# Scaling and casting w_out on GpSimd, with the second half requested by SyncE

## The chip, the cores and the metric

The kernel runs on one core of a Trainium2 chip. The metric is the device time of one execution in microseconds, the median of several. The engines are named as in the profile: PE is TensorE, DVE is VectorE, ACT is ScalarE, POOL is GpSimd, SP is SyncE.

## The reference

A global filter along the sequence (a real Fourier transform, a product with a complex filter, the inverse transform) is followed by two dense layers with a snake activation between them.

```
x: (8, 3008, 256); filt_r, filt_i: (1505, 256)
X = rfft(x, axis=1); Y = X * (filt_r + 1j * filt_i); y = irfft(Y, n=3008, axis=1)
x2 = y.reshape(24064, 256)
h = x2 @ w_in                              # w_in: (256, 2048)
s = sin(alpha * h)                         # alpha: (2048,)
g = h + s * s / (alpha + 1e-09)
out = g @ w_out                            # w_out: (2048, 256), out: (24064, 256) float32
```

## The kernel before

The work is split by linearity. Since g has a part that is linear in h, the kernel computes out = (s * s) @ (w_out / alpha) + x2 @ (w_in @ w_out). The first factor on the right is held as `w_out2` (float16, 16 blocks of 128 rows), the product w_in @ w_out as `m_t`. For `m_t` it needs w_out itself in float16, `w_out16`, and the transpose of w_in, `w_inT`.

The Fourier transform is done as small matrix products in stages (`f1`, `f2x`, `product`, `f2g`, `f3`), one pass for each of the 8 sequences of the batch. The first sequence is worked alone on the chip (`f1_chip`, `turn1`, `g_chip`, `turn2`); it is the prologue. The other seven are cut into small steps which a hand-written table, `plan`, puts into slots of the main loop. The main loop runs over 47 chunks g of 512 tokens with 8 slots q each. In slot 8 * g + q stand, in this order: one `mlp_in` (two matmuls into a bank of the pool `psh`, and the sine on ACT), a part of `mlp_out` of the chunk before (matmuls with `w_out2` as the moving side, L290), the planned steps, a second `mlp_in` and a second part of `mlp_out`; in every second slot `square` on DVE (L278) squares four blocks of the sine. The order on every engine is that of the code; each engine works through its queue in that order and waits at an instruction until its inputs are there.

w_out comes in two halves of 1024 rows, in float32, into one staging buffer: the pool `stp` has one buffer under the tag `st`, which both halves and later the two halves of w_in in float32 share in turn. So the second half can be requested only when all readers of the first are done. `load_w_out(h, eng)` (L346) requests half h on the queue of `eng`; `prep_w_out(h, k)` (L354) scales four of its blocks by `recip`, which is 1 / (alpha + 1e-9), on DVE; `cast_w_out(h)` (L351) casts the half on POOL. The first half is requested in the prologue on SP's queue, after the first half of w_in has landed. Its cast, its two `prep_w_out` and the request of the second half on POOL's queue stand in slots 6 and 7; the second half is scaled and cast in slot 10, and `prep_m` (L373) multiplies w_in by w_out16 in slot 13. `mlp_out` of chunk 0 uses blocks 0 to 15 of `w_out2` in turn, from slot 8 on.

In the same slots stand the steps of the second sequence: from slot 5 to slot 10 up to three `f1` steps each (L141, into a bank of the pool `psf` of three; even steps are evicted by ACT, odd ones by DVE, L142), and one `prep_w_inT` (L367, another `psf` bank, evicted by ACT and DVE in turn, L370). After `f1` steps 7 and 15 SP stores `asb` to DRAM (L146); `shuffle1` reads it back from slot 10 (L196). `load_x(1, 4)` puts eight loads on POOL's queue at the end of the prologue.

Of the kernel before, what the change touches and what calls it, by code (L numbers as in the profile page):

```python
# [63 lines left out]
def kernel(  # L64
# [10 lines left out]
    nc = tc.nc  # L75
# [3 lines left out]
    def dram(ap, off, dims):  # L79
        return bass.AP(tensor=ap.tensor, offset=ap.offset + off, ap=dims)  # L80
# [34 lines left out]
    w_out2 = cpool.tile([128, 16, C], FP16, name="w_out2")  # L115
# [5 lines left out]
    def gate(ins, earlier):  # L121

        tc.add_manual_dep(ins.ins, earlier.ins.name, mybir.DependencyInfo(
            mybir.DependencyClass.Sync, mybir.DependencyReason.DATA), reason="order of transfers")

    def load_x(b, parts=2):

        xt[b] = (xbpool if b else vpool).tile([GT, RP, C], FP16, name="xt", tag="xb" if b else "vt")
        n = RP // parts
        for h in range(parts):  # L130
            for p0, p1 in ((0, 80), (80, GT)):
                x_dma[b, h] = nc.gpsimd.dma_start(  # L132
                    out=xt[b][p0:p1, n * h:n * h + n, :],
                    in_=dram(x, (b * S + RP * p0 + n * h) * C, [[RP * C, p1 - p0], [1, n * C]]))
# [14 lines left out]
    def f1_chip(k):  # L149

        for half in range(2):
            ps = (psf if half else psh).tile([128, 4, 4 * NK], FP32, name="psa0", tag="f" if half else "ph")
            for i in range(4):
                nc.tensor.matmul(out=ps[:, i, :], lhsT=xt[0][:, 4 * k + i, 128 * half:128 * half + 128],
                                 rhs=wa2, start=True, stop=True)
            (nc.vector.tensor_copy if half else nc.scalar.copy)(
                out=a_c[:, half, :, 16 * k:16 * k + 16].rearrange("p s (r a) -> p s r a", a=4),
                in_=ps.rearrange("p r (s a) -> p s r a", a=4))
# [154 lines left out]
    def evict_out(g, h):  # L313
        if h == 0:
            ot[g] = opool.tile([128, 4, C], FP32, name="ot", tag="ot")
        nc.vector.tensor_copy(out=ot[g][:, 2 * h:2 * h + 2, :], in_=po[g, h])  # L316
# [20 lines left out]
    w_inT, w_out32, w_in32, alpha_b = [], [], [], []  # L337

    def prep_alpha():
        ps = pso.tile([128, 2, C], FP32, name="psal", tag="po")  # L340
        nc.tensor.matmul(out=ps[:, 0, 0:16], lhsT=alpha_r, rhs=ident32, start=True, stop=True)
        nc.vector.tensor_copy(out=alpha_t, in_=ps[:, 0, 0:16])
        nc.vector.tensor_scalar(out=recip, in0=alpha_t, scalar1=1e-9, scalar2=None, op0=ALU.add)
        nc.vector.reciprocal(out=recip, in_=recip)
# [6 lines left out]
    def cast_w_out(h):  # L351
        nc.gpsimd.tensor_copy(out=w_out16[:, 8 * h:8 * h + 8, :], in_=w_out32[h])

    def prep_w_out(h, k):  # L354
        for i in range(4 * k, 4 * k + 4):
            nc.vector.tensor_scalar(out=w_out2[:, 8 * h + i, :], in0=w_out32[h][:, i, :],  # L356
                                    scalar1=recip[:, 8 * h + i:8 * h + i + 1], scalar2=None,
                                    op0=ALU.mult)

# [32 lines left out]
    def keep_busy(n, src):  # L392

        ps = psh.tile([128, 2, C], FP32, name="idle", tag="ph")
        for _ in range(n):
            nc.tensor.matmul(out=ps, lhsT=ident[0:src.shape[0]], rhs=src, start=True, stop=True)

    def load_filter(s0, n, earlier=None):

        for f, src in ((0, filt_r), (1, filt_i)):  # L400
            first = nc.gpsimd.dma_start(out=fri[0:32, f, s0:s0 + n, :],
                                        in_=dram(src, s0 * C, [[MT * C, 32], [C, n], [1, C]]))
            if earlier is not None and f == 0:
                gate(first, earlier)
            filter_dma[s0] = nc.gpsimd.dma_start(
                out=fri[32:64, f, s0:s0 + n, :],
                in_=dram(src, (MT - s0) * C, [[MT * C, 32], [-C, n], [1, C]]))
# [10 lines left out]
    def swap_wg(s0, n):  # L418

        cs = slice(128 * s0, 128 * s0 + 128 * n)  # L420
        for p in (0, 64):
            nc.vector.tensor_copy(out=wgs[p:p + 64, cs], in_=wg[64 - p:128 - p, cs])
# [3 lines left out]
    def at(slot, f, *args):  # L426
        plan.setdefault(int(slot), []).append((f, args))
# [25 lines left out]
        for q, u in zip(slots, todo):  # L453
            at(8 * g + q, f3, *u)
    for k in range(2):
        at(6 + k, prep_w_out, 0, k)
        at(10 + k, prep_w_out, 1, k)
        at(13, prep_m, k)
    at(6, cast_w_out, 0)
    at(7, load_w_out, 1, nc.gpsimd)  # L460
    at(10, cast_w_out, 1)
    at(14, load_w_in32, 0)
    at(22, load_w_in32, 1)
    for k in range(8):
# [6 lines left out]
    with tc.manual_schedule():  # L471
        nc.sync.dma_start(out=wa2, in_=wa2_d.ap())
        nc.sync.dma_start(out=ident, in_=id_d.ap())
        nc.scalar.dma_start(out=alpha_r, in_=moe_alpha.rearrange("(a p) -> a p", p=128))
        nc.scalar.dma_start(out=ident32, in_=id32_d.ap())
        nc.scalar.dma_start(out=we2, in_=we2_d.ap())
        nc.scalar.dma_start(out=wa, in_=wa_d.ap())
        nc.scalar.dma_start(out=we, in_=we_d.ap())
        nc.sync.dma_start(out=wb[:, 0:8 * 128], in_=wb_d.ap()[:, 0:8 * 128])
        warm = cpool.tile([128, 1], FP32, name="warm")  # L480
        nc.vector.memset(warm, 0.0)
        nc.scalar.activation(out=warm, in_=warm, func=AFT.Sin)
        load_x(0, 4)
        for s0 in (0, 8, 16):
            load_filter(s0, 8, None if s0 else x_dma[0, 1])
        for h in range(2):
            hs = slice(1024 * h, 1024 * h + 1024)
            for cb in range(2):
                w_in_dma[h, cb] = nc.gpsimd.dma_start(out=w_in16[:, cb, hs],
                                                      in_=moe_w_in[128 * cb:128 * cb + 128, hs])  # L490
        gate(nc.sync.dma_start(out=wg[:, 0:8 * 128], in_=wg_d.ap()[:, 0:8 * 128]), x_dma[0, 2])
        nc.sync.dma_start(out=wb[:, 8 * 128:], in_=wb_d.ap()[:, 8 * 128:])
        gate(nc.sync.dma_start(out=wg[:, 8 * 128:], in_=wg_d.ap()[:, 8 * 128:]), filter_dma[0])
        a_c = vpool.tile([128, 2, NK, 128], FP16, name="a_c", tag="vt")
        prep_alpha()
        for k in range(8):
            f1_chip(k)
            if k == 0:
                keep_busy(3, xt[0][:, 0:2, :])
        bint[0] = xbpool.tile([128, NK, C], FP16, name="bint", tag="xb")  # L500
        wgs = vpool.tile([128, NK * 128], FP16, name="wgs", tag="vt")
        b_c = agpool.tile([128, 2, RP, NK, 4], FP16, name="b_c", tag="ag")
        for t in range(12):
            turn1(t)
            if t in (2, 4, 6, 8, 10, 11):
                f2x(0, (t - 1) // 2)
            if t == 9:
                swap_wg(0, 8)
                fold_filter(0, 8)
        for t in range(16):  # L510
            if t in (4, 8):
                fold_filter(2 * t, 8)
                if t == 4:
                    swap_wg(8, 16)
            if t >= 4:
                g_chip(t // 2 - 2, t % 2)
                if t % 2 and t > 8:
                    keep_busy(2, wg[:, 0:512])
            if 4 <= t < 10:
                f2x(0, t + 2)  # L520
            if t < 12 and t % 2:
                product(0, t // 2, 0)
        gin[0] = ginpool.tile([4 * NK, RP, C], FP16, name="gin", tag="gin")
        for j in range(4):
            turn2(j)
        gate(load_w_out(0, nc.sync), w_in_dma[0, 1])
        load_x(1, 4)
        for i in range(4):
            f3(i // 2, i % 2)

        for g in range(NCH):
            for q in range(8):
                if g and q == 7:
                    evict_out(g - 1, 0)
                mlp_in(g, 2 * q)
                if g:
                    mlp_out(g - 1, q, 1)
                for f, args in plan.get(8 * g + q, ()):
                    f(*args)
                mlp_in(g, 2 * q + 1)  # L540
                if g:
                    mlp_out(g - 1, q, 0)
                if g and q == 7:
                    evict_out(g - 1, 1)
                    store_out(g - 1, 0, 4, (nc.sync,))
                if q % 2:
                    square(g, q)
        out_last(NCH - 1)
# [28 lines left out]
```

## Time and profile before

| what | us |
|---|---|
| median of 3 runs | 839.96 (838.85 to 840.75) |
| the profiled execution | 839.08 |
| its span, first to last instruction | 837.3 |
| PE busy | 813.0 (97%) |
| ACT busy | 620.3 (74%) |
| DVE busy | 515.2 (62%) |
| POOL busy | 36.3 (4%) |

The span and the busy times are those of the profiled execution. The granted clock of PE is 0.997 of full speed over the span. The chain that ended last is 90% PE. The slots in question lie between 48 and 80 us of the span; the chunk loop begins at 39.5 us.

A row of a timeline has the start, the length, the engine, the line, the operation with its tiles, and in brackets the idle time of the engine ahead of it with what ended that. Numbers at the end of names of buffers are left out, so `w_out` stands for `w_out2`, `w_out16` and `w_out32` alike.

### The profile page before, as it was taken

The numbers are of one execution on the slowest core, as the hardware profiler recorded it, in microseconds if no ns is written. First come the engines' busy times: TensorE is split into PE (matmuls) and PEld (weight loads), VectorE is DVE, ScalarE is ACT, GpSimd is POOL, SyncE is SP. The second block draws the span as 40 slices with busy tenths as digits, with TensorE's granted clock in tenths as the row PEclk, the third lists the DMA queues.
The fourth block names the chain that finished last, engine by engine and source line by source line (L and its number), as shares of the span: only waits on it lengthen the run. The fifth ranks groups of instructions, "written<-read, shape, count | busy, mean of one in ns | idle before, by whom it ended". The sixth has DMA issues, their size and how long they took to land.

```text
span 837.3 us, 15277 instructions
## 1 busy us (share of the span) xinstructions
PE 813.0 (97%) x6221; PEld 573.7 (69%) x6221; DVE 515.2 (62%) x683; ACT 620.3 (74%) x1155; POOL 36.3 (4%) x66
## 2 busy tenths in 40 slices
PE   6779999999999999999999999999999999999997
PEld 5547676677767776677767776677766777767665
DVE  4886975676466665566555684567655675443532
ACT  4786987787777786788777887778877787666662
POOL 5301000000000000000000000000000000000000
PEclk9999999999999999999999999999999999999999
DMA  9926385424644163612834146431645233321122
GB/s 197 208 66 244 103 192 113 139 73 103 152 102 126 51 161 89 201 29 75 196 92 140 51 107 169 103 101 51 160 117 144 61 96 95 61 52 26 28 50 50
DMA packets 68134, 91.55 MB, mean 109 GB/s; under 512 B 7224, under 2 KB 52808, under 8 KB 66552
## 3 DMA queue, kind: packets, MB, share of 16 engines
q1 hardware_dynamic: 61792, 71.25, 30.8%
q0 software_dynamic: 5760, 19.14, 11.2%
q8 instruction: 48, 0.79, 0.4%
q10 hardware_dynamic: 512, 0.19, 0.1%
q14 instruction: 22, 0.18, 0.1%
HBM read 58.83 MB, written 46.66 MB: 126 GB/s over the span
## 4 chain that ended last, share of the span: by engine, by line
PE 90%; DVE 5%; DMA 3%; issue 1%; POOL 1%; ACT 0%; DVEq 0%; POOLq 0%
PE po L290 42%; PE ph L271 37%; PE psa L141 2%; PE psy L260 2%; PE psg L232 2%; PE psx L202 2%; DMA w_out<-in_moe_w_out_dram 1%; DVE vt L278 1%; PE pe L304 1%; DMA fri<-in_filt_i_dram 1%; DMA xt<-in_x_dram 1%; DVE gin L189 1%; DVE w_out L356 1%; PE psg L175 0%; DVE z L215 0%
## 5 line engine op out<-in xcount | busy, mean ns | idle before, releaser
L273 ACT ACTIVATE vt<-ph 128x512 f16<-128x512 f32 x688 | 404.5, 601 | 141.9 <-PE ph L271 136.8
L290 PE MATMUL po<-w_out,vt 128*128 128x256 f16 x2944 | 426.6, 272 | 1.4 <-DVE ot L316 0.8
L290 PEld LDWEIGHTS <-vt 128*128 128x128 f16 x2944 | 287.4, 98 | 173.4 <-issue 2.2
L271 PE MATMUL ph<-yt,w_ina 128*128 128x512 f16 x1376 | 399.3, 379 | 0.0
L278 DVE TENSOR_TENSOR vt<-vt 128x2048 f16<-128x2048 f16 x188 | 230.1, 1224 | 196.6 <-ACT vt L273 196.0
L271 PEld LDWEIGHTS <-w_ina 128*128 128x128 f16 x1376 | 128.2, 98 | 32.8
L316 DVE COPY ot<-po 128x512 f32<-128x512 f32 x92 | 63.0, 688 | 22.4 <-PE po L290 21.4
L206 ACT CAST xs<-psx 128x512 f16<-128x512 f32 x96 | 56.6, 592 | 8.2 <-PE psx L202 8.0
L142 DVE CAST asb<-psa 96x512 f16<-96x512 f32 x56 | 38.2, 685 | 33.4 <-PE psa L141 31.6
L234 ACT CAST gsb<-psg 128x512 f16<-128x512 f32 x84 | 49.5, 589 | 12.3 <-PE psg L232 11.2
L290 PE MATMUL po<-m_t,yt 128*128 128x256 f16 x368 | 55.2, 273 | 0.0
L264 DVE CAST yt<-psy 128x240 f16<-128x240 f32 (+45 forms) x92 | 32.2, 351 | 34.3 <-ACT yt L262 33.3
L262 ACT CAST yt<-psy 128x376 f16<-128x376 f32 (+29 forms) x128 | 46.2, 363 | 7.6 <-PE psy L260 0.7
L273 ACT ACTIVATE vt<-ph,alpha_t 128x512 f16<-128x512 f32 x64 | 42.8, 694 | 11.1 <-PE ph L271 10.8
L260 PE MATMUL psy<-we,gin 96*128 96x94 f16 x512 | 42.1, 204 | 1.1 <-ACT asb L142 0.7
L132 POOL DMA_DIRECT2D xt<-in_x_dram x40 | 20.9, 528 | 496.2 <-PE psy L260 287.5
L260 PEld LDWEIGHTS <-gin 96*128 96x128 f16 x512 | 35.6, 97 | 7.7 <-issue 1.5
L290 PEld LDWEIGHTS <-yt 128*128 128x128 f16 x368 | 36.0, 98 | 4.2
L142 ACT CAST asb<-psa 96x512 f16<-96x512 f32 x56 | 32.3, 583 | 8.0 <-PE psa L141 7.9
L202 PE MATMUL psx<-bint,wb 128*128 128x256 f16 x192 | 37.4, 277 | 0.0
L271 PE MATMUL ph<-yt,w_in 128*128 128x512 f16 x128 | 36.4, 379 | 0.2 <-ACT yt L262 0.2
L215 DVE TENSOR_TENSOR z<-xs,fri 128x1024 f16<-128x1024 f16 x48 | 32.9, 686 | 4.6 <-ACT xs L206 4.5
(71 smaller groups left out, 384.1 us busy)
## 6 DMA issues: line engine op xcount, KB each, us to landing
out_dram<-ot SPq DMA_DIRECT2D x109, 128.0 KB
scr<-asb SPq DMA_DIRECT2D x14, 768.0 KB
bint<-scr SPq DMA_DIRECT2D x21, 512.0 KB
scr<-gsb SPq DMA_DIRECT2D x21, 512.0 KB
xt<-in_x_dram POOLq DMA_DIRECT2D x12, 640.0 KB, 8.1
gin<-scr SPq DMA_DIRECT2D x7, 768.0 KB
out_dram<-ot SPq DMA_DIRECT2D x84, 60.0 KB
gin<-scr SPq DMA_DIRECT2D x7, 576.0 KB
```

The costliest lines, as they stand in the source:

```text
L142: (nc.vector.tensor_copy if u % 2 else nc.scalar.copy)(out=asb[b][:, 2 * u:2 * u + 2, :], in_=ps)
L202: nc.tensor.matmul(out=ps[:, i, :], lhsT=wb[:, 128 * (2 * t + i):128 * (2 * t + i) + 128], rhs=bint[b][:, 2 * t + i, :], start=True, stop= ...
L206: nc.scalar.copy(out=xs[b, t // 2][:, t % 2 * 2:t % 2 * 2 + 2, :], in_=ps)
L215: nc.vector.tensor_tensor(out=z[k], in0=xs[b, k], in1=fri[:, 0, k4, :], op=ALU.mult)
L234: nc.scalar.copy(out=gsb[b][:, 2 * t:2 * t + 2, :], in_=ps)
L260: nc.tensor.matmul(out=ps[:, t, :], lhsT=gin[b][:, 4 * a + t, 128 * cb:128 * cb + 128], rhs=we if b else we2, start=True, stop=True)
L262: nc.scalar.copy(out=yt[g][:, cb, :, lo:lo + n], in_=ps[:, :, 0:n])
L271: nc.tensor.matmul(out=ph, lhsT=(w_in16 if g < 4 else w_ina)[:, cb, 128 * jb:128 * jb + 128], rhs=yt[g][:, cb], start=(cb == 0), stop=(cb ...
L273: nc.scalar.activation(out=vt[g][:, jb, :], in_=ph, func=AFT.Sin, scale=alpha_t[:, jb:jb + 1] if g < 4 else 1.0)
L278: nc.vector.tensor_tensor(out=v4, in0=v4, in1=v4, op=ALU.mult)
L290: nc.tensor.matmul(out=po[g, h][:, i, :], lhsT=vt[g][:, k, ts] if k < 16 else yt[g][:, k - 16, t], rhs=w_out2[:, k, :] if k < 16 else m_t[ ...
L316: nc.vector.tensor_copy(out=ot[g][:, 2 * h:2 * h + 2, :], in_=po[g, h])
```

## The change

`prep_w_out` scales a whole half, eight blocks, on POOL instead of four on DVE. The scaling and the cast of the first half stand in the prologue, behind the loads of the second sequence on POOL's queue. The request of the second half stands in slot 1 on SP's queue, and its scaling and cast in slot 1 on POOL. In both halves the scaling is now ahead of the cast.

```
-    def prep_w_out(h, k):
-        for i in range(4 * k, 4 * k + 4):
-            nc.vector.tensor_scalar(out=w_out2[:, 8 * h + i, :], in0=w_out32[h][:, i, :],
+    def prep_w_out(h):
+        for i in range(8):
+            nc.gpsimd.tensor_scalar(out=w_out2[:, 8 * h + i, :], in0=w_out32[h][:, i, :],
                                     scalar1=recip[:, 8 * h + i:8 * h + i + 1], scalar2=None,
                                     op0=ALU.mult)
...
     for k in range(2):
-        at(6 + k, prep_w_out, 0, k)
-        at(10 + k, prep_w_out, 1, k)
         at(13, prep_m, k)
-    at(6, cast_w_out, 0)
-    at(7, load_w_out, 1, nc.gpsimd)
-    at(10, cast_w_out, 1)
+    at(1, load_w_out, 1, nc.sync)
+    at(1, prep_w_out, 1)
+    at(1, cast_w_out, 1)
...
         gate(load_w_out(0, nc.sync), w_in_dma[0, 1])
         load_x(1, 4)
+        prep_w_out(0)
+        cast_w_out(0)
         for i in range(4):
             f3(i // 2, i % 2)
```

## The prediction

> **What bounds the kernel now.** I read the page first: TensorE (PE) is busy 97% of the span at full granted clock, so a change pays only where PE stands idle. The stretches of busy time say where that is near the changed code.
>
> ```profile
> 50.00:55.00 5.00, 3.65 (x25) 2.08 (x25) 4.07 (x10) 3.95 (x8) 0.00 (x0) 1.00 0.00 0
> 55.00:60.00 5.00, 3.47 (x25) 1.90 (x23) 4.79 (x11) 4.11 (x9) 0.96 (x1) 1.00 0.57 144
> 60.00:65.00 5.00, 4.76 (x38) 3.19 (x36) 2.94 (x5) 3.68 (x7) 0.00 (x0) 1.00 0.71 218
> 65.00:70.00 5.00, 4.38 (x40) 3.12 (x39) 4.22 (x9) 3.44 (x6) 1.90 (x1) 1.00 0.62 165
> 70.00:75.00 5.00, 5.00 (x51) 4.14 (x49) 2.87 (x5) 2.63 (x6) 0.00 (x0) 1.00 0.68 247
> ```
>
> The columns are length, then busy time of PE, weight loads, VectorE (DVE), ScalarE (ACT) and GpSimd (POOL). From 50 to 70 us PE is idle 1.35 + 1.53 + 0.24 + 0.62 = 3.74 us; from 70 to 100 it is full. So a microsecond that PE wins before 70 should reach the end, and there are fewer than four to win. The chain of waits through this window:
>
> ```profile
> 54.29 1.05 DVE w_out L356 x4
> 55.34 0.64 DVE asb L142
> 55.98 1.06 DVE w_out L356 x4
> 57.06 0.54 issue
> 57.61 8.66 DMA w_out<-in_moe_w_out_dram
> 66.29 2.08 DVE w_out L356
> 68.42 0.64 PE po L290 x4
> ```
>
> VectorE scales the first half of w_out late (slots 6 and 7), which frees the staging buffer late, so the second half is requested at 57.61, lands 8.66 us later, and is scaled while PE already wants it. Twelve microseconds of chain, but PE worked beside it. What PE really lost is in its own timeline (the bracket is idle time and who ended it):
>
> ```profile
> 56.26 0.38 PE L367 MATMUL pst<-ident,w_in 128*128 128x128 f16 x4 [0.79 <-ACT asb L142]
> 58.90 0.38 PE L367 MATMUL pst<-ident,w_in 128*128 128x128 f16 x4 [0.74 <-ACT asb L142]
> 62.12 0.38 PE L367 MATMUL pst<-ident,w_in 128*128 128x128 f16 x4 [0.24 <-ACT asb L142]
> 68.42 0.64 PE L290 MATMUL po<-w_out,vt 128*128 128x256 f16 x4 [0.62 <-DVE w_out L356]
> ```
>
> Only 0.62 us of it is w_out. The other gaps end on ScalarE evictions. Last, the two kinds of w_out work, and POOL's and DVE's timelines where they meet:
>
> ```profile
> L356 DVE TENSOR_SCALAR w_out<-w_out,recip x16: 336/341/2070, 54.2 to 69.9; 128x256 f16<-128x256 f32 x16
> L352 POOL CAST w_out<-w_out x2: 1896/1900/1903, 36.2 to 66.3; 128x2048 f16<-128x2048 f32 x2
> ```
>
> ```profile
> 36.23 1.90 POOL L352 CAST w_out<-w_out 128x2048 f16<-128x2048 f32 x1
> 66.32 1.90 POOL L352 CAST w_out<-w_out 128x2048 f16<-128x2048 f32 x1 [7.75 <-DMA w_out<-in_moe_w_out_dram]
> ```
>
> ```profile
> 47.41 1.23 DVE L278 TENSOR_TENSOR vt<-vt 128x2048 f16<-128x2048 f16 x1 [0.43 <-ACT vt L273]
> 51.70 1.23 DVE L278 TENSOR_TENSOR vt<-vt 128x2048 f16<-128x2048 f16 x1 [0.46 <-ACT vt L273]
> 57.83 1.23 DVE L278 TENSOR_TENSOR vt<-vt 128x2048 f16<-128x2048 f16 x1 [0.21 <-ACT vt L273]
> 66.29 3.90 DVE L356 TENSOR_SCALAR w_out<-w_out,recip 128x256 f16<-128x256 f32 x8 [0.78 <-DMA w_out<-in_moe_w_out_dram]
> ```
>
> Fifteen of the 16 scalings take some 0.34 us. The other one, 2.07, began at 66.29 beside the POOL cast at 66.32 to 68.22 and ended with it: 1.73 us in which a DVE instruction stood still for a POOL one. That is the 0.62 us that PE lost.
>
> **Removed.** VectorE loses 16 scalings: 8 x 0.34 = 2.7 us at 54.2 to 57.0, the 2.07 at 66.29, and 7 more up to 70.2. From the last group PE gains its 0.62 us wait. From the first group little: the eviction asb at 55.29, between the two fours, began when its matmul was done (the three psa matmuls start at 54.66, 0.22 apart, 0.38 each: the second ends at 55.26), so it was not delayed. But the order of the built instructions shows one change of buffers: the transpose at 56.26, which took the bank of the eviction that ScalarE ended at 56.20, takes in the changed kernel the bank that this VectorE eviction frees at 55.98, and starts some 0.06 later, as at 56.26: 56.04, so 0.22 us earlier. ScalarE's next activation waited 0.42 us for PE at 57.11 and follows; the gaps at 58.90 and 62.12 only move along. Gain 0.62 + 0.22 = 0.84.
>
> **Added on POOL.** Behind the last x load (issued by 36.23) stand one code-library reload that the build puts ahead of the first scaling, then 8 scalings, the cast, and after the transfer 8 more and a cast. No row shows a reload. POOL's shortest row, a memset, is 0.10 us; the longest landing of a load it issued is 8.7. I take 8.7 for the reload R, as it too must fetch something. A scaling t costs at least the cast's rate, 1900 / 2048 x 256 = 0.24 us, and at most the whole cast's 1.90; I take 0.24, an instruction of the same engine and types, a row short of which only fixed cost is missing.
>
> The request now stands on SyncE's queue behind the first cast; behind it there wait the asb stores (first issued at 56.23). The request leaves at 36.2 + R + 8t + 1.9 = 48.7, so SyncE is free in time, and the transfer runs in a stretch with a DMA share of 0.00. I keep the 8.66 us landing all the same; the request itself took 0.42 us on SyncE. The first scaled block of the second half is ready at 36.2 + R + 8t + 1.9 + 0.4 + 8.7 + t = 47.2 + R + 9t = 58.1. PE needs it at 68.42 - 0.62 - 0.22 = 67.6. The cover holds while R + 9t stays below 20.4. The cast second half, for the product m, is ready at 49.1 + R + 16t = 61.6; PE wants it at about 72.4. So POOL's slowness costs nothing directly.
>
> **The new collision.** By these values POOL scales at 44.9, casts at 46.8 to 48.7, and works again at 57.8 to 61.7, beside the squares (L278), which come about every 4.2 us. Whether a square stands still for POOL as the scaling did is not shown; the bounds are 0 and 1.73 us a meeting, or 3.5 for two. The squares at 47.41 and 51.70 are in front of evictions that PE waits for (PE idles 0.29 us at 50.12 and 0.48 at 53.57 for DVE asb), so a delay there is on the path; after the one at 57.83 DVE has 1.45 us idle to absorb it. Since R is not known, I place the cast at random: a square meets it with chance 1.9 / 4.2 = 0.45 and then waits half of it, 0.95, which is 0.43; a scaling adds at most 0.24, mostly less. I take 0.5.
>
> [...]
>
> [...]
>
> **Sum.** Profiled execution: span 837.3 and 839.08 in all. 839.08 - 0.62 - 0.22 + 0.50 = 838.74. The median of the runs, 839.96, lies 0.88 above the profiled one, so 839.6. A measurement here tells about 0.2% (1.7 us) from no change, so this is no measurable change.
>
> **Rivals.**
> Slower, by lateness: if R + 9t passes 20.4, PE stalls again at the first block of the second half, one for one. R of 24 with t of 0.24 gives 5.8 us, 839.1 + 5.8 = 844.9; t of 1.5 with R of 8.7 gives 1.8 at once and, since each later block comes 1.5 us after the last, more. SyncE's asb stores would also be held from R above 16. For it: the extra instruction, unseen here; against: a slack of 9.5 us. Chance 0.18.
> Slower, by collision: the first cast and a scaling burst each hold one of the early squares for the full 1.73: 839.1 + 3.5 = 842.6. It decides where the cast lands within 1.2 us before a square. Chance 0.15.
> Faster: the squares are not held, and the two ScalarE gaps close with VectorE's 2.7 us of relief, beyond my 0.22: 0.57 + 0.74 + 0.24 = 1.5 more. 838.24 - 1.5 + 0.88 = 837.6. Against it: those rows name ACT, not DVE. Chance 0.17.
> The request is early but hidden anyway: that is half of my forecast already, since PE lost only 0.62 us of the 8.66.
>
> **Numbers.** Forecast case 0.50, from 838.3 to 841.6. Range for 8 in 10: 838.0, a part of the faster case, to 843.5, both collisions and a mild lateness.
>
> **What would show it.** Right: no wait of PE on w_out at 68; the transfer of the second half landed before 60; the transpose near 56.0 waiting on DVE; SyncE's first asb store unmoved. Collision: a square longer than 1.23 us or late beside a POOL row. Lateness: PE waiting on POOL at po (L290), and idle POOL time ahead of the first scaling above 16 us. Wrong: a saving of over 1.7 us before 70 us, or any new PE gap after it.

## The result and the profile after

The changed kernel takes 841.34 us (median of 20 runs, 838.36 to 843.91) against 839.92 us for the kernel before on the same chip (20 runs, 838.85 to 840.75). The ratio is 1.0015, with a 95% interval of 1.0008 to 1.0022: slower by 1.4 us, where no measurable change, with a small gain in the sum, was forecast. The profiled execution has a span of 842.1 us and took 843.91 us, the longest of its 20; its parts are read here, not its total.

First the rows of PE that answer to the three gaps and the wait on w_out of before (timeline of the changed kernel; start, length, work, and in brackets the idle time ahead with what ended it):

```profile
49.82 0.38 PE L187 MATMUL pst<-ident,b_c 128*96 128x128 f16 x4 [3.16 <-DVE gin L189]
...
61.92 0.38 PE L367 MATMUL pst<-ident,w_in 128*128 128x128 f16 x4 [0.56 <-DVE asb L142]
64.55 0.38 PE L367 MATMUL pst<-ident,w_in 128*128 128x128 f16 x4 [0.74 <-ACT asb L142]
67.78 0.38 PE L367 MATMUL pst<-ident,w_in 128*128 128x128 f16 x4 [0.24 <-ACT asb L142]
```

The last three are as forecast: the transpose now takes the bank that DVE freed and waits 0.56 instead of 0.79, the next two gaps only moved along, and no row waits for w_out any more. The first one is new. The same transposes of `turn2` stood at 45.24 before, behind 0.49 us of idle time, and the first square on DVE ahead of them was undisturbed (kernel before, timelines of PE and DVE):

```profile
45.24 0.38 PE L187 MATMUL pst<-ident,b_c 128*96 128x128 f16 x4 [0.49 <-DVE gin L189]
```

```profile
43.37 1.21 DVE L278 TENSOR_TENSOR vt<-vt 128x2048 f16<-128x2048 f16 x1
```

In the changed kernel POOL's timeline and DVE's first square say what came between:

```profile
39.00 7.25 POOL L356 TENSOR_SCALAR w_out<-w_out,recip 128x256 f16<-128x256 f32 x8
46.20 1.88 POOL L352 CAST w_out<-w_out 128x2048 f16<-128x2048 f32 x1
```

```profile
45.28 3.89 DVE L278 TENSOR_TENSOR vt<-vt 128x2048 f16<-128x2048 f16 x1
```

The square of the first chunk took 3.89 us instead of 1.21 (43.37 to 44.58 before). It was recorded from 45.28, behind it the cast ran from 46.20 to 48.08, and the square ended at 49.17, which is 1.09 us after the cast: so it seems to have done its work when the cast was over. The chain of waits carries it (start, length, what):

```profile
42.28 3.08 DVE gin L189 x5
45.35 3.81 DVE vt L278
49.17 1.21 DVE gin L189 x2
```

The evictions of `turn2` that PE waited for (gin, L189) stood behind it on DVE's queue.

What each part cost is read from stretches between landmarks of PE's work: the first matmul of `mlp_in` (ph, L271) in the chunk loop (39.52 before, 41.42 after), the transposes behind the held square (45.24, 49.82), the next transposes for `prep_w_inT` (50.12, 56.01), the ones whose bank was swapped (56.26, 61.92), the place where `mlp_out` came to the second half of w_out (68.89, 73.72), and the first product of `prep_m` (72.38, 77.22). The first four stretches, before (first fence) and after (second); the columns are those of the prediction, and the third number from the end is the granted clock:

```profile
39.52:45.24 5.72, 5.13 (x46) 3.32 (x46) 5.57 (x10) 4.23 (x8) 0.00 (x0) 1.00 0.39 76
45.24:50.12 4.88, 4.08 (x31) 2.27 (x31) 4.40 (x7) 4.40 (x9) 0.00 (x0) 1.00 0.01 3
50.12:56.26 6.14, 4.12 (x26) 2.18 (x26) 5.25 (x12) 5.09 (x11) 0.00 (x0) 1.00 0.00 0
56.26:68.89 12.63, 11.03 (x84) 7.29 (x84) 9.58 (x15) 9.49 (x16) 2.86 (x2) 1.00 0.70 193
```

```profile
41.42:49.82 8.40, 5.13 (x47) 3.32 (x46) 8.25 (x10) 4.62 (x8) 6.67 (x7) 1.00 0.45 87
49.82:56.01 6.19, 5.42 (x31) 3.15 (x31) 4.42 (x7) 4.56 (x9) 2.54 (x3) 0.72 0.46 154
56.01:61.92 5.91, 4.12 (x27) 2.18 (x27) 3.97 (x6) 4.63 (x9) 5.91 (x7) 1.00 0.00 0
61.92:73.72 11.80, 10.82 (x84) 7.29 (x84) 7.00 (x9) 9.38 (x17) 1.32 (x1) 1.00 0.38 99
```

| stretch | before | after | difference | what it is |
|---|---|---|---|---|
| first | 5.72 | 8.40 | +2.68 | the held square |
| second | 4.88 | 6.19 | +1.31 | 31 matmuls busy 5.42 instead of 4.08, clock 0.72 |
| third | 6.14 | 5.91 | -0.23 | the swapped bank |
| fourth | 12.63 | 11.80 | -0.83 | no wait on w_out |
| fifth | 3.49 | 3.50 | +0.01 | nothing |

Together +2.94. The rest of the longer span, 842.1 - 837.3 = 4.8, is the prologue, which in this execution reached the loop 1.90 later (41.42 against 39.52); in the profiles below the loop begins between 39.41 and 40.77, and in two more of the changed kernel itself at 39.77 and 39.60. So most of it looks like scatter of this one execution; a small part that the change causes is not excluded.

### The profile page after: what moved, and what is told of

Same layout as the page of the kernel before. It is cut to its first block, busy times and chain, and to the rows that moved or that the text cites. A ratio compares the mean times of both kernels' runs of the same rounds, so it can differ in the third digit from the quotient of the medians.

```text
span 842.1 us, 15279 instructions
## 1 busy us (share of the span) xinstructions
PE 815.2 (97%) x6221; PEld 575.4 (68%) x6221; DVE 512.3 (61%) x667; ACT 620.9 (74%) x1155; POOL 50.4 (6%) x81
## 4 chain that ended last, share of the span: by engine, by line
PE 91%; DVE 4%; DMA 2%; ACT 1%; issue 1%; POOL 1%; DVEq 0%; ACTq 0%; POOLq 0%
PE po L290 42%; PE ph L271 37%; PE psa L141 3%; PE psy L260 2%; PE psx L202 2%; PE psg L232 2%; DVE vt L278 1%; PE pe L304 1%; DMA fri<-in_filt_r_dram 1%; DMA xt<-in_x_dram 1%; PE psg L175 1%; DVE gin L189 1%; PE psm L376 0%; DVE z L215 0%; DVE t L222 0%
## 5 line engine op out<-in xcount | busy, mean ns | idle before, releaser
L271 PE MATMUL ph<-yt,w_ina 128*128 128x512 f16 x1376 | 399.2, 379 | 0.0
L278 DVE TENSOR_TENSOR vt<-vt 128x2048 f16<-128x2048 f16 x188 | 232.8, 1238 | 197.3 <-ACT vt L273 196.8
L271 PEld LDWEIGHTS <-w_ina 128*128 128x128 f16 x1376 | 128.2, 98 | 32.8
L271 PE MATMUL ph<-yt,w_in 128*128 128x512 f16 x128 | 37.6, 390 | 0.2 <-ACT yt L262 0.2
```

The source lines that it names most:

```text
L271: nc.tensor.matmul(out=ph, lhsT=(w_in16 if g < 4 else w_ina)[:, cb, 128 * jb:128 * jb + 128], rhs=yt[g][:, cb], start=(cb == 0), stop=(cb ...
L278: nc.vector.tensor_tensor(out=v4, in0=v4, in1=v4, op=ALU.mult)
```

## The experiments

Theory A: the loop gains about 1 us as the change intends, and loses more because the first cast on POOL holds the first square. Theory B: the loss lies elsewhere and the square is beside it. Theory C: POOL holds DVE up as long as its queue holds work, so the scalings count as well as the cast. Once the granted clock had shown itself, theory A1: the idle time behind the hold makes the clock dip, which is a second price of the same hold.

**Cast ahead of the scalings, in both halves.** POOL then casts before the loop begins; by theories B and C the time stays at the changed kernel's 841.3.

```
+        cast_w_out(0)
         prep_w_out(0)
-        cast_w_out(0)
...
     at(1, load_w_out, 1, nc.sync)
+    at(1, cast_w_out, 1)
     at(1, prep_w_out, 1)
-    at(1, cast_w_out, 1)
```

> The changed kernel with the cast ahead of the eight scalings on POOL, in both halves; nothing else differs. Theory A (a square that meets POOL work waits for the POOL instruction in progress, and the 1.9 us cast is the one that costs): the cast now runs in the 2 us after the x loads, before the first square, and the first square meets a scaling of 0.92 us at most. The square of 3.89 us shrinks to 2.2 or less, the idle of PE ahead of the fourth group of transposes shrinks from 3.2 us to 1.4 or less, and the time falls to between 838.9 and 840.2. [...]

Measured 839.29 us (838.22 to 844.05, 12 runs), ratio 0.9998 (0.9986 to 1.0009). The cast ran from 37.13 to 39.04 and the first square took 1.21 us (timelines of POOL and DVE):

```profile
37.13 1.91 POOL L352 CAST w_out<-w_out 128x2048 f16<-128x2048 f32 x1
```

```profile
44.27 1.21 DVE L278 TENSOR_TENSOR vt<-vt 128x2048 f16<-128x2048 f16 x1
```

From the loop's start to the first product of `prep_m` it was 72.23 - 40.42 = 31.81, against 32.86 before: 1.05 less, the gain that the third and fourth stretch give (0.23 + 0.83). The loss is gone with the meeting. Three of the 12 runs lay at 840.6 to 844.1; why is not known. The second cast met a square here (at 52.6; the cast took 2.96 us, the square 1.23).

**Without the first square**, in the changed kernel and, as a control, in the kernel before.

```
-                if q % 2:
+                if q % 2 and (g, q) != (0, 1):
```

> The changed kernel without the first square of chunk 0 (four of its 16 blocks of the sine stay unsquared). To be read against the kernel before with the same square left out. Theory A: with the square that was held gone, nothing that PE waits for stands beside the cast, but the second square may meet the end of it; this kernel is 0.2 to 1.1 us faster than its control. Theory B (late prologue) and any theory in which the square has no part: it is 1.4 us slower than its control, as the changed kernel is against the one before.

> The control: the kernel before without the first square of chunk 0 (four of its 16 blocks of the sine stay unsquared). The square stands in the chain that PE waits for at 45 us (1.13 us of it), so this kernel should be 0 to 1.2 us faster than the kernel before under every theory.

Measured 838.37 us (ratio 0.998, 0.9972 to 0.9989) for the changed kernel and 839.40 (0.9991, 0.9982 to 1.0) for the one before. With the square away from both, the change gains 1.03 us. Leaving it out gains the changed kernel 3 us and the kernel before less than one. Theory B falls.

**Bursts on POOL late in the loop of the kernel before**, gated on a square, in chunks with nothing else on POOL: 16 scalings, 6 casts, 8 scalings and a cast, 6 memsets, 16 scalings.

```
+        if g in (40, 44):
+            for c in range(16):
+                scale(c)              # 128x256, as in prep_w_out
+        elif g == 41:
+            for c in range(6):
+                cast(c)               # 128x2048, as in cast_w_out
+        elif g == 42:
+            for c in range(8):
+                scale(c)
+            cast(0)
+        else:                         # six memsets of 128x2048
```

> The kernel before, with bursts of POOL work set behind the first square of chunks 40 to 44, where nothing waits for POOL: 16 scalings, 6 casts back to back, 8 scalings and a cast, 6 memsets of the same size as a cast's output, 16 scalings. Read are the durations of the squares (1.22 us undisturbed), PSUM evictions on DVE (0.69) and POOL's own. Theory A: squares beside casts take up to 1.9 us longer, one cast each, squares beside scalings up to 0.9, beside memsets nothing or less, evictions nothing. Theory C: a square beside the six casts waits for the rest of the burst, up to 9 us. If squares are not lengthened at all, both fall. The time should be within 2 us of the kernel before.

Measured 839.75 us. DVE's squares beside the first 16 scalings (which began at 723.45; the longest one there), the single cast and the memsets:

```profile
726.20 1.52 DVE L278 TENSOR_TENSOR vt<-vt 128x2048 f16<-128x2048 f16 x1 [2.85 <-ACT vt L273]
...
764.96 2.48 DVE L278 TENSOR_TENSOR vt<-vt 128x2048 f16<-128x2048 f16 x1 [0.37 <-ACT vt L273]
...
771.86 1.23 DVE L278 TENSOR_TENSOR vt<-vt 128x2048 f16<-128x2048 f16 x1 [2.86 <-ACT vt L273]
```

and POOL's rows of the casts:

```profile
740.44 14.06 POOL L292 CAST fri<-w_in 128x2048 f16<-128x2048 f32 x6
...
764.48 1.89 POOL L292 CAST fri<-w_in 128x2048 f16<-128x2048 f32 x1
```

The square at 764.96 met one cast (764.48 to 766.37) and ended at 767.44, 1.07 after it. In the row of six casts two squares took 1.93 and 2.51 us and two more 5.71 together: each waits for one cast or a part of it, not for the row, and the casts themselves grow from 1.89 to 2.34 us each. Beside scalings the longest square was 1.52, beside memsets none grew. Theory C falls; the partner that counts is a single cast.

**The changed kernel twice more**, unchanged, for the spread of the hold.

> The changed kernel once more, for a second profile. The first had a square of 3.89 us beside the last scaling and the cast, but it was also the run with the longest time of 20 (843.91; median 841.34). Theory A (the time of a run follows from where POOL's first cast falls against the first two squares): a run near 841 has a first or second square lengthened by 1 to 2.7 us, a run near 838.5 has none, and the stretch from the first chunk matmul to the product m is 31.8 us (without any) plus what the squares lost. Theory B (the prologue): that stretch is the same in every run and the runs differ ahead of it.

> The changed kernel a third time, under the same two theories: by A the stretch from the first chunk matmul to the product m is 31.8 us plus what the first squares lost to POOL, and by B it is the same in every run.

Measured 841.81 and 838.22 us, and the two profiles differ in just this. In the first the square was held again (timeline of DVE, then of POOL):

```profile
43.63 3.17 DVE L278 TENSOR_TENSOR vt<-vt 128x2048 f16<-128x2048 f16 x1
```

```profile
43.83 1.88 POOL L352 CAST w_out<-w_out 128x2048 f16<-128x2048 f32 x1
```

Its stretches are longer than those of before by 1.95, 1.32, -0.23 and -0.82, together 2.2. In the second, POOL waited 1.56 us for the first half of w_out, and the cast, at 45.57, came after the square (same two views):

```profile
43.45 1.38 DVE L278 TENSOR_TENSOR vt<-vt 128x2048 f16<-128x2048 f16 x1
```

```profile
37.87 7.75 POOL L356 TENSOR_SCALAR w_out<-w_out,recip 128x256 f16<-128x256 f32 x8 [1.56 <-DMA w_out<-in_moe_w_out_dram]
```

There the same way took 71.57 - 39.60 = 31.97 us, 0.89 less than before, at full clock. In these three profiles, whether the first half lands before POOL is free goes with a loss of 2.2 to 2.9 or a gain of 0.9. The 20 runs fit two such groups: five lie at 838.4 to 839.9, the other fifteen at 840.9 and more. The record has each run's mean granted clock: 0.993 or 0.994 in eleven of the fifteen and 0.997 or 0.998 in four, 0.995 to 0.997 in the five. So a lower clock goes with the longer group in most of its runs, but not in all; which of these runs had a held square is not shown, as only one left a profile.

**Idle matmuls against the dip.** Twelve matmuls with no use (`keep_busy`, already in the kernel's prologue) in slot 3 of the changed kernel, to fill PE's idle time.

```
+    at(3, keep_busy, 12, wg[:, 0:512])
```

> The changed kernel with 12 idle matmuls (2.6 us at full clock) on PE in slot 3, ahead of the transposes that waited 3.16 us for the held square; their result is not used. Theory A1 (the granted clock of 0.72 that followed, and the 1.3 us that it cost, came from PE's standing idle): the clock stays at 1.00 after the gap, and runs with a held square are 1.3 us shorter than they were; runs without one are up to 2.6 us longer, since the idle matmuls then stand in the way; the slowest runs fall from 843.9 to about 842.5. Theory A2 (the clock's dip has another cause and comes by chance): the dip stays, and the time rises by 0 to 2.6 us.

Measured 840.73 us (839.67 to 841.5, 11 runs), ratio 1.001 (1.0001 to 1.0019). In its profile the first half came 1.98 us late and nothing was held, so it says nothing on the clock. No run was above 841.5, where A1 forecast 842.5 for the slowest and A2 no such fall; without a profile of a held square this does not decide.

**Cast first in the first half only.** The version to which the runs so far point.

```
+        cast_w_out(0)
         prep_w_out(0)
-        cast_w_out(0)
```

> The changed kernel with the cast ahead of the scalings in the first half only; in the second the scalings stay ahead. With both halves turned round most runs were 838.2 to 839.5, but three of 12 were 840.6 to 844.1, and the profile showed the second cast (52.6 us) and the third square (52.6) meeting on the start. Theory A: here the first cast ends 5 us before the first square and the second cast falls after 60 us, where DVE has idle time, so no cast meets a square that PE waits for: median 838.6 to 838.9, ratio 0.9985 to 0.999, and no run over 840.5. If the outliers stay, they have another cause than the second cast.

Measured 838.82 us (838.24 to 840.78, 11 runs), ratio 0.999 (0.9981 to 0.9999): faster than both kernels, against the one before if by little. One run, 840.78, was above the 840.5 that theory A allowed; its cause is not known. POOL's cast is over 5 us before the first square, which began at 44.55 and took 1.21:

```profile
37.41 1.91 POOL L352 CAST w_out<-w_out 128x2048 f16<-128x2048 f32 x1
```

The first two stretches have the lengths of the kernel before, 5.72 and 4.88, at a clock of 1.00.

**Making the meeting certain.** Four kernels were to force the hold, with and without idle matmuls, so that the dip could be priced. In the first pair the cast waits for the fourth sine of the first chunk, as the square does, and the scalings stand behind it; in the second pair the eighth scaling waits for the third sine, with the cast right behind.

```
+        if h == 0:
+            gate(ins, sine[0, 3])                # first pair: ins is the cast
...
+            if (h, i) == (0, 7):
+                gate(ins, sine[0, 2])            # second pair: ins is the eighth scaling
...
+    at(3, keep_busy, 8, wg[:, 0:512])            # the second kernel of each pair
```

> The changed kernel with the first cast held back until the fourth sine of chunk 0 is done, which is what the first square waits for too, and the eight scalings of the first half behind the cast. So cast and first square start together in every run, whenever the first half of w_out landed. Theory A: the square is held for 1.5 to 1.9 us in every run, PE idles 2.0 to 2.4 us ahead of the fourth group of transposes, the granted clock dips behind it as in two of the three profiles of the changed kernel (1.3 us), and with the gain of 1.05 the time is 839.85 + 1.8 + 1.3 - 1.05 = 841.9, in 841 to 842.5, with a narrower spread than the changed kernel's 5.5 us. Were the square not held, 838.8.

> The same with 8 idle matmuls (1.7 us at full clock) on PE in slot 3, just ahead of the transposes that wait for the held square; their result is not used. They fit into the 2.0 to 2.4 us gap. Theory A1 (the dip of the granted clock comes from PE's standing idle in the gap): the clock stays at 1.00, the stretch of 6.2 us behind the gap takes 4.9 again, and the time is 1.0 to 1.5 us below the kernel without them, 840.4 to 840.9. Theory A2 (the dip comes from something else): no difference, within 0.4 us.

> The kernel before this missed: with the cast alone, started from a wait together with the square, the square was not held and the cast took 3.02 us instead. In the two profiles with a held square the cast had stood right behind a scaling that was in progress when the square came. Here that is made the rule: the eighth scaling of the first half waits for the third sine of chunk 0, so that it runs as the first square becomes ready, and the cast stands right behind it. Theory A, mended (a cast queued behind a running POOL instruction goes ahead of a DVE square that waits): the square is held to the end of the cast in nearly every run, about 2.0 us; PE idles 2.5 us; the clock dips (1.3 us); 839.6 + 2.0 + 1.3 - 1.05 = 841.9, in 841.3 to 842.5, spread under 2.5 us. Rival (the hold in two of three profiles was chance, each tie may fall either way): a mix of 838.6 and 841.9 as in the changed kernel.

> The same with 8 idle matmuls (1.7 us at full clock) on PE in slot 3, ahead of the transposes that wait for the held square; their result is not used. They fit into the gap. Theory A1 (the dip of the granted clock comes from PE's standing idle in the gap): the clock stays at 1.00, the stretch behind the gap takes 4.9 us instead of 6.2, and the time is 1.0 to 1.5 us below the kernel without them, 840.4 to 840.9. Theory A2 (the dip comes from something else): no difference, within 0.4 us.

Measured 838.63 (ratio 0.999, 0.9981 to 0.9999), 839.57 (1.0, 0.9991 to 1.0009), 839.08 (0.9992, 0.9983 to 1.0001) and 839.40 (0.9994, 0.9986 to 1.0003). All four missed: no square was held. In the first kernel the two started 0.06 us apart, and it was POOL that waited (timelines of DVE and POOL):

```profile
44.56 1.21 DVE L278 TENSOR_TENSOR vt<-vt 128x2048 f16<-128x2048 f16 x1
```

```profile
44.50 3.02 POOL L353 CAST w_out<-w_out 128x2048 f16<-128x2048 f32 x1 [7.07 <-ACT vt L273]
```

The cast ended 1.75 us after the square; in the third kernel it was the same (square 43.96 to 45.17, cast 44.13 to 46.92, again 1.75 after). With nothing held there was no dip to fill, and with the eight matmuls the median of the first pair rose by 0.94 us and that of the second by 0.32, which is within the scatter.

**A longer POOL instruction.** Between the sixth and the seventh scaling of the changed kernel a copy of 128x4096 float16 that nobody reads; then the same with idle matmuls.

```
-        prep_w_out(0)
+        prep_w_out(0, range(6))
+        nc.gpsimd.tensor_copy(out=w_ina, in_=w_in16)
+        prep_w_out(0, range(6, 8))
...
+    at(3, keep_busy, 10, wg[:, 0:512])           # the second kernel only
```

> The kernel before this missed: with a wait on the last scaling the first square was not held either, so a tie is not won by order alone. Here the hold is made certain: on POOL, between the sixth and the seventh scaling of the first half, stands a copy of 128x4096 float16 that nothing uses (about 3.8 us at the cast's rate), so that it is in the middle when the first square comes. Theory A: the square waits to the end of the copy, 1.8 to 2.6 us (up to 3.8 where the first half lands late), PE idles 2.3 to 3.1 us, and the granted clock dips behind it: 839.7 + 2.2 + 1.3 - 1.05 = 842.2, in 841.5 to 843. If the hold does not bring the dip: 840.9. If the queued scalings and cast pass the waiting square, it is held 3.7 us longer still, 845 or more.

> The same with 10 idle matmuls (2.2 us at full clock) on PE in slot 3, ahead of the transposes that wait for the held square; their result is not used. They fit into the gap of 2.3 us or more. Theory A1 (the dip of the granted clock comes from PE's standing idle in the gap): the clock stays at 1.00, the stretch behind the gap takes 4.9 us instead of 6.2, and the time is 1.0 to 1.5 us below the kernel without them. Theory A2 (the dip comes from something else): no difference, within 0.4 us.

Measured 842.14 us (841.1 to 844.54, ratio 1.0028, 1.0018 to 1.0038) and 841.13 (840.24 to 843.1, 1.0016, 1.0007 to 1.0025). The square was held in both and took 3.61 and 3.50 us. In the first (timelines of POOL and DVE):

```profile
43.12 3.59 POOL L527 COPY w_ina<-w_in 128x4096 f16<-128x4096 f16 x1
```

```profile
44.63 3.61 DVE L278 TENSOR_TENSOR vt<-vt 128x2048 f16<-128x2048 f16 x1
```

It ended 1.53 us after the copy, beside the seventh and eighth scaling, so those held it little further and the cast, which began at 48.98, not at all. Without idle matmuls, the first fence's two stretches; with them, the second's:

```profile
40.77:48.88 8.11, 5.13 (x46) 3.32 (x46) 7.96 (x10) 4.61 (x8) 8.11 (x6) 0.96 0.34 66
48.88:54.67 5.79, 5.18 (x31) 2.87 (x31) 4.51 (x7) 4.13 (x8) 1.98 (x2) 0.76 0.46 123
```

```profile
39.41:47.41 8.00, 7.29 (x56) 4.30 (x56) 7.85 (x10) 4.61 (x8) 8.00 (x6) 1.00 0.27 52
47.41:52.30 4.89, 4.08 (x32) 2.27 (x32) 4.40 (x7) 4.02 (x8) 1.97 (x2) 1.00 0.31 76
```

The transposes behind the held square, first without idle matmuls, then with them:

```profile
48.88 1.18 PE L187 MATMUL pst<-ident,b_c 128*96 128x128 f16 x8 [2.88 <-DVE gin L189]
```

```profile
47.41 0.38 PE L187 MATMUL pst<-ident,b_c 128*96 128x128 f16 x4 [0.61 <-DVE gin L189]
```

The hold lengthens the first stretch alike (8.11 and 8.00 against 5.72). Where PE stood idle for 2.88 us in one piece, the clock of the next stretch is 0.76 and it takes 5.79; where idle matmuls left 0.61 us of it, the clock is 1.00 and it takes 4.89, as before. That is 0.90 us in the profile and 1.01 in the medians, whose two intervals overlap. One pair could be chance, but the 15 profiles whose PE rows reach over the first 20 us of the loop agree. In just three of them rows of four `mlp_in` matmuls grow there from 1.03 us to 1.47 and more, at 0.72, 0.76 and 0.72 of full clock, the ones where PE stood idle for 3.16, 2.88 and 2.44 us in one piece; in the other 12 they take 1.03 throughout, and the longest idle time is 0.79 us. So A1 holds and A2 falls: the idle time goes with the dip, and filling it removes the dip while the square is still held.

## Why the prediction was wrong, step by step

The time lies inside the range that was given, 838.0 to 843.5; the direction of the sum is what came out wrong. The prediction also took 1.7 us as the least that can be told from no change; with 20 runs of each, 1.4 us could be.

- **The gain was right and a little small.** 0.62 + 0.22 = 0.84 was forecast; 0.83 + 0.23 = 1.06 came, and 1.03 between the two kernels without the square. VectorE's relief did not close ScalarE's gaps (0.74 and 0.24 stayed), so the faster rival falls.
- **Lateness did not arise, as forecast, though both of its terms were off.** The reload R was taken at 8.7 us, which is too much, and the scaling t at 0.24, which is too little. No run shows a reload that fetches something, as R was taken to be: what the trace has ahead of the first scaling is two rows of 37 ns. The 16 scalings have a median of 922 ns:

```profile
L356 POOL TENSOR_SCALAR w_out<-w_out,recip x16: 914/922/1624, 39.0 to 60.5; 128x256 f16<-128x256 f32 x16
L356 POOLq MODIFY_POOL_CONFIG  x2: 37/37/37, 38.9 to 38.9; - x2
```

  The last load ended at 38.88 and the first scaling began at 39.00, so R is at most 0.12 of waiting there, and R + 9t = 0.12 + 8.3 = 8.4 where the forecast had 10.9, both far from 20.4. The request left at 48.11 and the scaling behind it began at 53.47, so it landed in 5.4 us, sooner than the 8.66 that the sum kept, with no wait of PE on it; SyncE's first `asb` store, at 62.1, waited for DVE's `asb` and not for the request.
- **The step that failed is the collision term, "I take 0.5".** It had a square that stands still for a POOL row, as in the runs, and three things wrong about it. First its place: "since R is not known, I place the cast at random" made it a chance of 0.45 against squares at 47.41 and 51.70, though by its own values the cast, at 46.8 to 48.7, lay on the square at 47.41. With the measured R and t the cast begins, on the clock of before, at 36.23 + 0.12 + 7.25 = 43.6, right on the square at 43.37, which the prediction did not look at, and whose followers on DVE are the evictions that PE waits for. Fifteen of the 20 runs are about as long as a held square makes them, not 45 in 100. Then its size: the hold was 2.68 and 1.95 us in the two held profiles, above the 1.73 that was the bound and far above the average of 0.95, because the square was recorded while scalings still ran and ended only 1.09 us after the whole cast. Last, what follows: PE's idle time of 3.16 and 2.44 us brought a clock of 0.72 and 1.3 us more, for which there was no term. With 0.5 for the collision the sum fell by 0.34 us; a held execution lost 1.95 + 1.32 or more there.
- **The sum with these terms.** For a held execution, 839.08 + 1.95 + 1.32 - 0.23 - 0.82 = 841.3 (measured 841.81 in that run), for one that is not held 839.08 - 0.9 = 838.2 (838.22). The median of 841.34 fits a mixture in which most executions are held. The collision rival had the right sign and mechanism at 842.6, but two meetings of 1.73 instead of one long one with its dip, and too small a chance.
- **Which rows held each other up.** What stood on POOL mattered: in the bursts single squares took up to 2.5 us beside casts, 1.23 beside memsets and at most 1.52 beside scalings. Where a square and a cast met, one ran through and the other seems to have done its work after (the square ended 1.07 to 1.09 us after the cast, or the cast 1.75 after the square). The one that was recorded first did not always win: the squares held in the two profiles of the changed kernel were recorded 0.92 and 0.20 us before the cast and lost, and the cast recorded 0.06 us before a square (44.50 and 44.56) lost too.

What stays open is who wins a near tie. A cast that stood in POOL's queue with no wait, behind scalings, won against a square that was recorded earlier, in two of two profiles. A cast with a wait of its own, or behind a scaling with one, lost, in the profiles of both forms. The runs do not show the cause.

## What to carry to other kernels

Work moved from VectorE to GpSimd was not free for VectorE here (a square of 3.89 us instead of 1.21): place each large GpSimd instruction on the time line with measured durations, look which VectorE instruction it lands on, and follow that one's queue to TensorE. Of two orders of the same GpSimd work, put the long instruction where VectorE has slack: one swapped line here turned +1.4 us into some -1.0 (838.82). And where the bounds of a start time are wide, check every meeting within them, not the ones near the middle value.

## What the runs showed of the hardware

- **Behind an idle time of 2.4 to 3.2 us in the loop TensorE's clock was halved for some 3.4 us,** in all three profiles that have one. In one-microsecond stretches behind the gap of the changed kernel, which ended at 49.82 (the one ahead of these and the one behind have 1.00):

```profile
50.82:51.82 1.00, 1.00 (x4) 0.37 (x3) 0.74 (x2) 0.54 (x2) 0.00 (x0) 0.63 1.08 383
51.82:52.82 1.00, 1.00 (x11) 0.92 (x10) 0.81 (x1) 0.83 (x3) 0.00 (x0) 0.50 0.87 306
52.82:53.82 1.00, 1.00 (x7) 0.55 (x6) 1.00 (x3) 0.76 (x3) 0.35 (x1) 0.50 0.07 19
53.82:54.82 1.00, 1.00 (x4) 0.48 (x3) 0.18 (x1) 0.66 (x1) 1.00 (x2) 0.66 0.00 0
```

  In stretches of 0.2 us the clock reads 1.00 up to 51.0, 0.50 from 51.2 to 54.4 and 1.00 again from 54.6. Taken to have only these two values, it was halved for (0.37 + 0.50 + 0.50 + 0.34) / 0.50 = 3.4 us, and it began more than 1 us after PE had started again. The same working gives 3.4 us behind the long copy, where it began before PE had started again (0.70 in the last idle microsecond), and 6.20 x 0.28 / 0.50 = 3.5 in the second stretch of the other held run of the changed kernel. In the prologue the dip did not always stand right behind such an idle time: in the kernel before, PE stood idle for 2.92 us up to 23.79 and the clock was 0.57 from 24 to 25; in the changed one it stood idle for 2.79 us up to 24.83 and the clock read 1.00 up to 30.
- **A small scaling on GpSimd cost far more than the cast's rate for its elements:** 0.92 us for 128x256 with a factor for each partition, against 1.88 for a cast of eight times as many.
